# Attention block plus channel MLP on one Trainium2 core: the head rebuilt slice by slice, two chunks turned by transfers, the MLP from the loop's top, the last sums kept on chip

## The chip, the cores and the metric

The kernel runs on one core of a Trainium2 chip. TensorE (PE in the profile, PEld for its weight loads) multiplies matrices into PSUM, VectorE (DVE) and ScalarE (ACT) do the elementwise work, GpSimd (POOL) a few small things, SyncE (SP) issues nearly all transfers. The metric is the device time of one execution in microseconds, a median over runs; lower is better.

## The reference, cut to what matters

```python
xn = layernorm(x)                                  # x: 1 x 2048 x 640
q, k, v = split(xn @ wqkv)                         # 32 heads of 20
o = softmax(q @ k.T * 20**-0.5) @ v
y = layernorm(xn)                                  # a second norm, for the MLP
h = gelu(y @ w1 + b1)                              # 640 -> 1536, tanh form
out = x + o.reshape(2048, 640) @ wo + h @ w2 + b2  # 1536 -> 640
```

All inputs and outputs are float32. The kernel multiplies float32 numbers as sums of half-precision parts: each operand is split into a high f16 part and an f16 remainder, and three of the four products are added in PSUM (`PASS`).

## The kernel before, in words

**Head (L155 to L509).** The 2048 tokens are worked off in four chunks of 512, the features in five slices of 128. For chunk c: `load_x` brings four blocks of 128 tokens x 640; `norm_a` (L220) takes mean and variance with DVE and starts the inverse root on GpSimd (L233, a power of -0.5); `norm_b` (L236) refines the root by one Newton step (L215 to L218) and scales the rows (L243); `norm_c` finishes a second root for the MLP's own norm and stores it in `rscr`. `transp` (L256) turns the scaled rows on PE so that features lie on partitions; `transp_out` (L266) copies the high part with ACT (L269) and the remainder with DVE (L270) into `xnt`, which is also written to DRAM (`xscr`) for the MLP. `qk(c, tt)` (L277) multiplies 256 columns of q and k by the chunk, 30 matmuls (L286); tt runs from 0 to 4. `qk_out` (L293) scales and splits the result with ACT (L300) and DVE (L301), squares it for the row norms (L304, L306) and writes it to `qkscr`, from where the attention loop reads stacked heads. `lengths` (L313) sums the squares by head on PE (L321). `vproj` (L343) and `vproj_out` make the V rows, four products a chunk. Between these steps stands the preparation of the weights: `sums` (squares with ACT, L94), `scale_of` (a PE sum over partitions, L110, and a chain of small DVE operations that make a power of two), `split_qkv` (L379: high part ACT L382, remainder DVE L383). `some(n)` advances the same for the MLP's weights.

The order of all this is written out by hand (L444 to L509, `manual_schedule`): every engine executes its instructions in the order in which the code names them. Before the first product `warm(40)` and `warm(12)` keep PE busy with matmuls whose result is not used. The staging of q and v lies in the tile of w1 and that of k in the tile of w2, so the loads of w2 (L474) and w1 (L482) wait until those are split. Each transfer has one of eight semaphores in turn, and its issue waits for the transfer eight before it. SP issues in order too: what waits at its front holds all behind it.

**Attention loop (L963 to L1008).** For 16 pairs of heads, two halves of the queries, two columns of 512 and 16 blocks of 128 keys: `scores` (L594) makes two matmuls (L600) and one ACT exponential of 128 x 1024 (L602); `rest` subtracts the bf16 upper part for half of the blocks (L614); `pv` (L619) adds the products with V (L631), four blocks late. When a column is done ACT copies the sums out (L652) and `unload` (L660) writes them to DRAM (`opart`, and the row sums to `lpart`). `finish` (L683) reads back two or three pairs at a time, divides, splits and writes `oscr`.

PE's other work is woven in by a credit: once in every group of four key blocks (twice in the very first) the credit grows by `rate = 1.235` us, and `other()` (L970) takes steps from a generator until it is used up: first the MLP (`mlp`, L865: `layer1` L823, `gelu`, `layer2` L855), then the output projection (`projection`, L908, matmuls L932). The generator's first value is subtracted from the credit at the start:

```python
                credit = 0.0 - next(fill)        # L965
            load_chunk(0)                        # L866, in mlp()
            load_chunk(1)
            yield 2.0
```

`load_chunk` (L802) reads 256 tokens of `xscr` into a tile of the pool m2, which before exists only from the loop on, and broadcasts the MLP norm's factor (`r2f`). `tick` advances the side jobs, one step per call; a `yield` in a side job is one tick.

**Tail (from L1009).** After the last scores the rest of the projection runs, with one tick for every three matmuls. The last `finish` has its own form: a selection matmul (L735) spreads the inverse row sums over partitions; `W1 = 24` and `W2 = 17` ticks stand between its loads and the operations that use them. Projection pieces 4 to 7 need what it writes.

Of the kernel before, what the change touches and what calls it, by code (L numbers as in the profile page):

```python
# [42 lines left out]
def mha_mlp_kernel(tc, x, wqkv, wo, w1, b1, w2, b2, out):  # L43
# [4 lines left out]
    with (  # L48
# [3 lines left out]
        tc.tile_pool(name="st", bufs=2) as stp,  # L52
        tc.tile_pool(name="psS", bufs=3, space=PSUM) as psS,
# [99 lines left out]


        with tc.tile_pool(name="pa", bufs=2) as pa, tc.tile_pool(name="pa1", bufs=1) as pa1, tc.manual_schedule():  # L155
# [9 lines left out]
            def load_x(c):  # L165
                xts[c] = []
                for j in range(4):
                    xt = pa.tile([P, D], F32, tag="xt", name="xt", bufs=5)
                    nc.sync.dma_start(xt, x2[c * 512 + j * P : c * 512 + (j + 1) * P, :])
                    xts[c].append(xt)  # L170
# [7 lines left out]
            for q, n in enumerate("qkv"):  # L178
                if n == "v":
                    load_x(1)  # L180
                for k0, k1 in ((0, 3), (3, KD)):
                    nc.sync.dma_start(stage[n][:, k0:k1], wqkv_v[:, k0:k1, q * D : (q + 1) * D])
# [19 lines left out]
            brow = pa1.tile([H, S], F16, name="brow")  # L202
# [10 lines left out]
            def newton(dst, v, pref):  # L213
                t = pa.tile([P, 4], F32, tag=pref + "t", name=pref + "t")
                nc.vector.tensor_mul(t, dst, dst)  # L215
                nc.vector.tensor_mul(t, t, v)
                nc.vector.tensor_scalar(t, t, -0.5, 1.5, ALU.mult, ALU.add)
                nc.vector.tensor_mul(dst, dst, t)  # L218

            def norm_a(c):  # L220

                xt = xts[c]
                st = pa.tile([P, 4, 2, 6], F32, tag="st", name="st")
                mv = pa.tile([P, 4, 2], F32, tag="mv", name="mv")
                ve = pa.tile([P, 4], F32, tag="ve", name="ve")
                r = pa.tile([P, 4], F32, tag="r", name="r")
                r2 = pa.tile([P, 4], F32, tag="r2", name="r2")
                for j in range(4):
                    for i in range(2):
                        nc.vector.bn_stats(st[:, j, i, :], xt[j][:, i * 320 : (i + 1) * 320])  # L230
                    nc.vector.bn_aggr(mv[:, j, :], st[:, j])
                nc.vector.tensor_scalar(ve, mv[:, :, 1], EPS, None, ALU.add)
                nc.gpsimd.tensor_tensor(r, ve, nhalf, ALU.pow)  # L233
                rs[c] = mv, ve, r, r2

            def norm_b(c):  # L236
                mv, ve, r, r2 = rs[c]
                newton(r, ve, "a")

                nc.vector.tensor_mul(ve, r, r)  # L240
                nc.vector.tensor_scalar(r, r, 1024.0, None, ALU.mult)
                for j in range(4):
                    nc.vector.tensor_scalar(xts[c][j], xts[c][j], mv[:, j, 0:1], r[:, j : j + 1],  # L243
                                            ALU.subtract, ALU.mult)
                nc.vector.tensor_mul(ve, ve, mv[:, :, 1])
                nc.vector.tensor_scalar(ve, ve, EPS, None, ALU.add)
                nc.gpsimd.tensor_tensor(r2, ve, nhalf, ALU.pow)
# [8 lines left out]
            def transp(c, k0, pts):  # L256
                if k0 == 0:
                    xnts[c] = pa.tile([P, KD, 2, 512], F16, tag="xnt", name=f"xnt{c}")
                pt = psS.tile([P, 2, 512], F32, tag="s", name="pt")
                for j in range(4):  # L260
                    for k in range(min(2, KD - k0)):
                        nc.tensor.transpose(pt[:, k, j * P : (j + 1) * P],
                                            xts[c][j][:, (k0 + k) * P : (k0 + k + 1) * P], ident)
                pts.append((c, k0, pt))
# [9 lines left out]

            PASS = ((0, 0), (0, 1), (1, 0))

            def qk(c, tt):  # L277
                ps = psS.tile([P, 2, 512], F32, tag="s", name="qkp")
                order = [(i, k) for i in range(2) for k in range(KD)]
                if c + tt == 0:  # L280

                    order = [(i, k) for k in range(KD) for i in range(2)]
                for i, k in order:
                    q, mm = divmod(2 * tt + i, KD)
                    for n, (a, b) in enumerate(PASS):
                        nc.tensor.matmul(ps[:, i, :], wv[:, k, q, a, mm * P : (mm + 1) * P],  # L286
                                         xnts[c][:, k, b, :], start=(k + n == 0), stop=(k == KD - 1 and n == 2))
                return ps
# [4 lines left out]
            def qk_out(c, tt, ps):  # L293
# [3 lines left out]
                sq = pa.tile([P, 2, 512], BF16, tag="sq", name="sq", bufs=2)  # L297
                for i0, i1 in parts:
# [3 lines left out]
                                                   ALU.mult, ALU.subtract)  # L302
                if c == 0:
                    nc.scalar.activation(sq, hl[:, 0], AF.Square)  # L304
                else:
                    nc.vector.tensor_mul(sq, hl[:, 0], hl[:, 0])  # L306
                for s in range(2):
                    nc.sync.dma_start(
                        qkscr[s, 2 * tt * P : (2 * tt + 2) * P, c * 512 : (c + 1) * 512]
                        .rearrange("(i p) t -> p i t", p=P), hl[:, s])  # L310
                pend.extend((c, 2 * tt + i, sq[:, i]) for i in range(2))

            def lengths():  # L313

                for c, m, sq in pend:
# [10 lines left out]
                pend.clear()  # L326

            def shifts():
# [12 lines left out]
                nc.sync.dma_start(bscr[:H, :], brow)  # L341
# [37 lines left out]
            def split_qkv(n):  # L379
                q = "qkv".index(n)  # L380
                for k in range(KD):
                    nc.scalar.activation(wv[:, k, q, 0], stage[n][:, k], AF.Copy, scale=scales[n])  # L382
                    nc.vector.scalar_tensor_tensor(wv[:, k, q, 1], stage[n][:, k], scales[n], wv[:, k, q, 0],  # L383
                                                   ALU.mult, ALU.subtract)
# [59 lines left out]
            warm(40)  # L444
            norm_a(0)
            nc.gpsimd.memset(brow, KROW)
            sums("q", [stage["q"][:, 0:3], stage["q"][:, 3:]])
            norm_b(0)
            pts = []
            transp(0, 0, pts)  # L450
            scale_of("q")
            transp(0, 2, pts)
            transp(0, 4, pts)
            warm(12)
            for t in pts:
                transp_out(*t)
            split_qkv("q")
            nc.sync.dma_start(bscr[H : H + 1, :], brow[0:1, :])
            nc.sync.dma_start(b1t, b1.rearrange("(k p) -> p k", p=P))
            for c in range(4):  # L460
                nxt = c + 1 if c < 3 else None
                for tt in range(5):
                    ps = qk(c, tt)
                    lengths()

                    if c == 0:
                        if tt == 0:
                            sums("k", [stage["k"][:, 0:3], stage["k"][:, 3:]])
                            norm_c(0)
                            scale_of("k")  # L470
                        elif tt == 1:
                            split_qkv("k")
                            norm_a(1)
                            nc.sync.dma_start(w2t, w2.rearrange("(k p) n -> p k n", p=P))  # L474
                        elif tt == 2:
                            sums("v", [stage["v"][:, 0:3], stage["v"][:, 3:]])
                            norm_b(1)
                            scale_of("v")
                        elif tt == 3:
                            norm_c(1)  # L480
                            split_qkv("v")
                            nc.sync.dma_start(w1t, w1.rearrange("(k p) n -> p k n", p=P))  # L482
                    else:
                        if nxt and tt < 3:
                            (norm_a, norm_b, norm_c)[tt](nxt)
# [4 lines left out]
                    if nxt and tt >= 2:  # L490
                        pts = []
                        transp(nxt, 2 * (tt - 2), pts)
                        transp_out(*pts[0])
                if c + 2 < 4:
                    load_x(c + 2)
# [4 lines left out]
                for j in range(4):  # L500
                    ps = vproj(c, j)
                    lengths()
# [5 lines left out]
                    vproj_out(c, j, ps)  # L508
            some(99)  # L509


        with ExitStack() as scope:
# [3 lines left out]
            m2 = pool(name="m2", bufs=2)  # L516
# [143 lines left out]
            def unload(g, hf, ev):  # L660
                cols = slice(hf * 1024, (hf + 1) * 1024)
                for p in range(2):
# [12 lines left out]
            fins = []  # L675
# [7 lines left out]
            def finish(g0, g1, hf):  # L683
# [6 lines left out]
                yield  # L690
                for p in range(2):
                    go(lt[: nh * 16, p, :], lpart[p, hf, 2 * g0 : 2 * g1, :].rearrange("h (b t) -> (h b) t", t=64))
                for c0 in range(0, 1024, w):
# [18 lines left out]
                    o0, o1, rb = o0[: r1 - r0], o1[: r1 - r0], rb[: r1 - r0]  # L712
                    for p, o in enumerate((o0, o1)):
                        go(o, opart[p, r0:r1, cols])
# [87 lines left out]
            def load_chunk(mc):  # L802
                t0 = mc * MC
                xnt = m2.tile([P, KD, 2, MC], F16, tag="xnt", name="xm")
                r2f = m2.tile([P, MC], F32, tag="r2f", name="r2f")
                nc.sync.dma_start(xnt, xscr[:, :, :, t0 : t0 + MC])
# [58 lines left out]
            def mlp():  # L865
                load_chunk(0)  # L866
                load_chunk(1)
                yield 2.0
# [22 lines left out]
            def addup_out(ps, acc, t0, hf):  # L891
                cols = slice(hf * 320, (hf + 1) * 320)
                nc.vector.scalar_tensor_tensor(acc[:, cols], ps[:, :320], fo, acc[:, cols], ALU.mult, ALU.add)  # L893
                if hf == 1:
                    nc.sync.dma_start(out2[t0 : t0 + P, :], acc)
# [10 lines left out]
            W1, W2 = 24, 17  # L906
# [222 lines left out]
```

## Time and profile before

| | us |
|---|---|
| median of 3 runs (lowest, highest) | 1376.91 (1376.67, 1377.99) |
| time of the profiled execution | 1378.13 |
| its span | 1376.4 |
| PE, DVE, ACT busy in it | 1347.3, 1061.0, 1125.5 |
| first product of q (L286) starts | 21.02 |
| chunk 1, 2, 3 begin | 76.0, about 129, 182.3 |
| attention loop begins (first L600) | 232.72 |
| last PV product ends | about 1303 |
| last projection matmul ends | 1369.6 |

The profile is that of one execution; its times count from the start of its span. A group line gives line, engine, operation, output and inputs; a timeline line gives start and duration, and in brackets how long the engine had stood idle and what ended that. PE and DVE overlap, so shares do not add up. Two figures are of use throughout: 30 matmuls of `qk` take 6.6, a product of `vproj` 4.14.

### The profile page before, as it was taken

The page shows a single profiled execution, that of the slowest core. Times are in us where ns is not written, and L with a number is a line of the kernel's source. Part 1 is how long each engine was busy: PE and PEld are TensorE (multiplying, and loading weights), DVE is VectorE, ACT ScalarE, POOL GpSimd, SP SyncE. Part 2 cuts the span into 40 slices and gives each one's busy share as a digit, 9 for nine tenths or more (in the row PEclk, how much of TensorE's full clock was granted, in tenths as well). Part 3 has the DMA queues.
Part 4 walks back from the last instruction along what each step waited for, and adds up shares of the span by engine and source line. Part 5 has one row for each costly group of instructions (what it writes and reads, how often), then busy time and mean ns, then how long its engine had stood idle before and what let it go on. Part 6 is the DMA issues. An engine that isn't in the chain of part 4 may idle for free.

```text
span 1376.4 us, 29091 instructions
## 1 busy us (share of the span) xinstructions
PE 1347.3 (98%) x11711; PEld 599.3 (44%) x11711; DVE 1061.0 (77%) x1425; ACT 1125.5 (82%) x1282; POOL 32.6 (2%) x75
## 2 busy tenths in 40 slices
PE   8999998999999999999999999999999999999998
PEld 6555555443334333433343333343434434333375
DVE  6647753899778988788888778887978898898732
ACT  5644332999999999999999999999999999999700
POOL 2000000000000000000000000000000000000000
PEclk9999999999999999999999999999999999999999
DMA  9853413012113222213231123232123222244275
GB/s 266 226 187 115 99 58 114 3 33 62 52 38 100 81 76 68 70 47 82 67 99 40 47 66 89 64 83 62 41 57 113 73 76 77 65 135 119 89 235 177
DMA packets 92320, 125.68 MB, mean 91 GB/s; under 512 B 16905, under 2 KB 58569, under 8 KB 92178
## 3 DMA queue, kind: packets, MB, share of 16 engines
q1 hardware_dynamic: 89218, 117.14, 28.9%
q0 software_dynamic: 2304, 5.24, 2.2%
q8 instruction: 94, 1.54, 0.5%
q10 hardware_dynamic: 656, 1.36, 0.3%
q14 instruction: 48, 0.39, 0.1%
HBM read 80.84 MB, written 42.86 MB: 90 GB/s over the span
## 4 chain that ended last, share of the span: by engine, by line
PE 66%; DVE 8%; ACT 3%; DMA 2%; issue 2%; SPq 1%; DVEq 0%; ACTq 0%
PE o L631 26%; PE s L600 16%; PE py L855 11%; PE pu L823 9%; PE z L932 4%; DVE low L614 3%; ACT p L602 3%; DVE u L758 1%; DVE u L759 1%; DVE w L762 1%; DMA oscr<-oa 1%; DMA acc<-accscr 0%; DVE w L763 0%; DVE hT L770 0%; DVE u L768 0%
## 5 line engine op out<-in xcount | busy, mean ns | idle before, releaser
L602 ACT ACTIVATE p<-s 128x1024 f32<-128x1024 f32 x1024 | 973.9, 1043 | 46.2 <-PE s L600 38.9
L614 DVE TENSOR_TENSOR low<-p 128x1024 f16<-128x1024 f32 x512 | 610.6, 1218 | 162.4 <-ACT p L602 161.7
L631 PE MATMUL o<-p,vfull 128*32 128x512 bf16 (+1 forms) x4096 | 430.2, 493 | 0.0
L600 PE MATMUL s<-qs,ks 61*128 61x512 f16 x2048 | 317.3, 382 | 7.0 <-ACT p L602 5.5
L600 PEld LDWEIGHTS <-ks 61*128 61x128 f16 x2048 | 64.0, 94 | 294.4 <-issue 291.9
L823 PE MATMUL pu<-xm,w1t 128*128 128x256 f16 x1440 | 181.1, 275 | 3.8 <-DMA xm<-xscr 2.7
L855 PE MATMUL py<-w2t,hT 128*128 128x320 f16 x1152 | 178.6, 300 | 1.7 <-DVE u L758 1.1
L823 PEld LDWEIGHTS <-w1t 128*128 128x128 f16 x1440 | 131.5, 98 | 72.1 <-issue 57.8
L855 PEld LDWEIGHTS <-hT 128*128 128x128 f16 x1152 | 102.5, 98 | 89.3 <-issue 55.1
L286 PE MATMUL qkp<-xnt,wv 128*128 128x512 f16 x600 | 132.5, 379 | 0.2 <-DVE wv L383 0.2
L631 PEld LDWEIGHTS <-vfull 128*32 128x32 f16 x3072 | 60.4, 95 | 137.7 <-issue 106.3
L631 PE MATMUL o<-low,vfull 128*32 128x512 f16 x1024 | 103.5, 378 | 3.7 <-DVE low L614 3.7
L300 ACT ACTIVATE qkhl<-qkp,qks 128x1024 f16<-128x1024 f32 (+1 forms) x24 | 23.3, 971 | 82.9 <-PE qkp L286 65.4
L286 PEld LDWEIGHTS <-wv 128*128 128x128 f16 x600 | 58.1, 98 | 68.2 <-DVE wv L383 0.7
L631 PEld LDWEIGHTS o<-p,vfull 128*32 128x32 f32 x2048 | 62.1, 108 | 52.3
L932 PE MATMUL z<-w1t,ot 128*128 128x320 f16 x480 | 66.3, 299 | 1.4 <-DMA ot<-oscr 0.8
L349 PE MATMUL vp<-wv,xnt 128*128 128x320 f16 x480 | 66.6, 299 | 0.0
L932 PEld LDWEIGHTS <-ot 128*128 128x128 f16 x480 | 46.5, 98 | 21.9 <-issue 2.9
L349 PEld LDWEIGHTS <-xnt 128*128 128x128 f16 x480 | 46.5, 98 | 18.2
L893 DVE SCALAR_TENSOR_TENSOR acc<-z,sc,acc 128x320 f32<-128x320 f32 x32 | 17.5, 550 | 46.8 <-PE z L932 42.7
L301 DVE SCALAR_TENSOR_TENSOR qkhl<-qkp,qks,qkhl 128x1024 f16<-128x1024 f32 (+1 forms) x24 | 26.5, 1104 | 32.2 <-ACT qkhl L300 32.2
L652 ACT ACTIVATE ev<-o 128x512 f32<-128x512 f32 x64 | 39.5, 618 | 3.5 <-PE o L631 3.5
(168 smaller groups left out, 682.6 us busy)
## 6 DMA issues: line engine op xcount, KB each, us to landing
qkscr<-qkhl SPq DMA_DIRECT2D x40, 256.0 KB
opart<-ev SPq DMA_DIRECT2D x124, 80.0 KB
ks<-qkscr SPq DMA_DIRECT2D x120, 80.0 KB
qs<-qkscr SPq DMA_DIRECT2D x192, 40.0 KB
oa<-opart SPq DMA_DIRECT2D x32, 240.0 KB
xt<-in_A_x_dram SPq DMA_DIRECT2D x16, 320.0 KB
xscr<-xnt SPq DMA_DIRECT2D x4, 1280.0 KB
xm<-xscr SPq DMA_DIRECT2D x8, 640.0 KB
```

The source lines that it names most:

```text
L286: nc.tensor.matmul(ps[:, i, :], wv[:, k, q, a, mm * P : (mm + 1) * P], xnts[c][:, k, b, :], start=(k + n == 0), stop=(k == KD - 1 and n == 2))
L300: nc.scalar.activation(hl[:, 0, i0:i1], ps[:, i0:i1], AF.Copy, scale=a)
L301: nc.vector.scalar_tensor_tensor(hl[:, 1, i0:i1], ps[:, i0:i1], a, hl[:, 0, i0:i1], ALU.mult, ALU.subtract)
L349: nc.tensor.matmul(ps[:, hf, :320], xnts[c][:, k, a, j * P : (j + 1) * P], wv[:, k, 2, b, hf * 320 : (hf + 1) * 320], start=(n == 0), stop ...
L600: nc.tensor.matmul(ps[:, a, :], ks[64 * a : 64 * a + 61, kb * P : (kb + 1) * P], qs[64 * a : 64 * a + 61, cc * 512 : (cc + 1) * 512], star ...
L602: nc.scalar.activation(pt, ps, AF.Exp, scale=QS)
L614: nc.vector.tensor_sub(low, pt, upper(pt))
L631: nc.tensor.matmul(pv.o[32 * q : 32 * q + 32, :], src[:, v0 - PAD * (1 - q % 2) :][:, :32], t, start=q not in pv.begun, stop=last, skip_gr ...
L652: nc.scalar.activation(evs[g, hf][:, cc], pv.o, AF.Copy)
L823: nc.tensor.matmul(ps[:, i], w1v[:, k, (f + i) // 4, a, fo_ : fo_ + P], xnt[:, k, b, :], start=(n == 0), stop=(n == 3 * KD - 1))
L855: nc.tensor.matmul(ps[:, :320], hTs[mc][:, f, a, j * P : (j + 1) * P], w2v[:, f, b, hf * 320 : (hf + 1) * 320], start=(n == 0), stop=(n == ...
L932: nc.tensor.matmul(ps[:, :320], ot[:, k, a, j * P : (j + 1) * P], wov[:, k, b, h * 320 : (h + 1) * 320], start=(n == 0), stop=(n == 3 * KD ...
```

## The change

Seven things are edited.

1. The weights of q are loaded in five slices, and their squares are summed slice by slice. Chunk 0's root is a square root on ACT and a reciprocal on DVE in place of GpSimd's power; the factor 1024 moves into the Newton step; the second root's start is a function of its own (`norm_b2`) and comes later for chunk 0. The length row `brow` has a quarter of its size, is filled earlier and is repeated by the transfer that stores it.
2. Chunk 0 is turned block by block as its rows are scaled, with q's scale before the last block; then each feature slice is copied out and 256 columns of q's weights are split for it. The second product takes its features in the outer loop too, has k's scale in its middle, and the outputs of the first product and the other columns of q follow it; an exponential of one element stands ahead of these. `warm` is called with 37 and 5.
3. Chunk 1 is turned on PE between the V products of chunk 0. Chunks 2 and 3 are split as rows (ACT, DVE) and turned by eight transposing transfers from SP out of three row tiles in turn.
4. `lengths` runs twice a chunk (four entries, then up to ten), with the squares of odd products in another pool.
5. x blocks are loaded into tiles of the pool m2, which now exists from the start; the first two MLP inputs are loaded in chunk 3, and `mlp` yields 0.0 at its start.
6. The last pair's sums are not written to DRAM: `finish` reads them from the tile in SBUF with twelve transfers on ACT's queue (four of them the earlier pair's), and W1 and W2 are 12 and 9.
7. The last block of the output is stored in two halves, the first from ACT's queue.

```diff
-                    xt = pa.tile([P, D], F32, tag="xt", name="xt", bufs=5)
+                    if j % 2 == 0:
+                        pair = m2.tile([P, KD, 2, MC], F16, tag="xnt", name="xt").bitcast(F32)
+                        pair = pair.rearrange("p k s t -> p (k s t)")
+                    xt = pair[:, j % 2 * D : (j % 2 + 1) * D]
...
-                for k0, k1 in ((0, 3), (3, KD)):
+                for k0, k1 in ((k, k + 1) for k in range(KD)) if n == "q" else ((0, 3), (3, KD)):
...
-                nc.gpsimd.tensor_tensor(r, ve, nhalf, ALU.pow)
+                if c == 0:
+                    nc.scalar.activation(r, ve, AF.Sqrt)
+                    nc.vector.reciprocal(r, r)
+                else:
+                    nc.gpsimd.tensor_tensor(r, ve, nhalf, ALU.pow)
...
+            def turn(c, j):
+                if j == 0:
+                    xnts[c] = pa.tile([P, KD, 2, 512], F16, tag="xnt", name=f"xnt{c}")
+                xv = xts[c][j].rearrange("p (k n) -> p k n", k=KD)
+                row = pa.tile([P, KD, 2, P], F16, tag="row", name="row", bufs=3)
+                nc.scalar.activation(row[:, :, 0, :], xv, AF.Copy)
+                nc.vector.tensor_sub(row[:, :, 1, :], xv, row[:, :, 0, :])
+                nc.sync.dma_start(xnts[c].rearrange("p k s t -> p (k s) t")[:, :, j * P : (j + 1) * P],
+                                  row.rearrange("p k s n -> p (k s n)"), transpose=True)
+                if j == 3:
+                    nc.sync.dma_start(xscr[:, :, :, c * 512 : (c + 1) * 512], xnts[c])
+                    del xts[c]
...
-            warm(40)
+            warm(37)
             norm_a(0)
-            nc.gpsimd.memset(brow, KROW)
-            sums("q", [stage["q"][:, 0:3], stage["q"][:, 3:]])
+            sums("q", [stage["q"][:, k] for k in range(KD)])
             norm_b(0)
-            pts = []
-            transp(0, 0, pts)
-            scale_of("q")
-            transp(0, 2, pts)
-            transp(0, 4, pts)
-            warm(12)
-            for t in pts:
-                transp_out(*t)
-            split_qkv("q")
...
+            for j in range(4):
+                if j == 3:
+                    scale_of("q")
+                    pt.append(psM.tile([P, 512], F32, tag="m", name="pt4"))
+                for k in range(KD - 1):
+                    nc.tensor.transpose(pt[k][:, j * P : (j + 1) * P], xts[0][j][:, k * P : (k + 1) * P], ident)
+            for j in range(4):
+                nc.tensor.transpose(pt[4][:, j * P : (j + 1) * P], xts[0][j][:, 4 * P :], ident)
+            warm(5)
+            for k in range(KD):
+                nc.scalar.activation(xnts[0][:, k, 0, :], pt[k], AF.Copy)
+                nc.vector.tensor_sub(xnts[0][:, k, 1, :], pt[k], xnts[0][:, k, 0, :])
+                split_qkv("q", [k], 0, 2 * P)
...
+                    if c == 0 and tt == 1:
+                        norm_b2(0)
+                        norm_c(0)
+                        nc.scalar.activation(junk[:, :1], ones[:, :1], AF.Exp)
+                        ps = qk(0, 1, lambda: scale_of("k"))
+                        hl = qk_out(0, 0, first)
+                        split_qkv("q", c0=4 * P)
+                        split_qkv("k")
...
-                    if nxt and tt >= 2:
-                        pts = []
-                        transp(nxt, 2 * (tt - 2), pts)
-                        transp_out(*pts[0])
+                    if nxt and c > 0 and tt >= 2:
+                        for j in ((0,), (1, 2), (3,))[tt - 2]:
+                            turn(nxt, j)
+                    if c == 3 and tt == 2:
+                        early = [load_features(mc) for mc in range(2)]
...
+                        for k in ((), (0,), (2, 4), ())[j]:
+                            transp(1, k, pts)
...
+                direct.extend([ev] if (g, hf) == ORDER[-1] else [])
-                for p in range(2):
+                for p in range(0 if direct else 2):
...
-                yield 2.0
+                yield 0.0
...
-                if hf == 1:
+                if t0 + P == S:
+                    (nc.scalar, nc.sync)[hf].dma_start(out2[t0 : t0 + P, cols], acc[:, cols])
+                elif hf == 1:
...
-            W1, W2 = 24, 17
+            W1, W2 = 12, 9
```

## The prediction

> **What bounds the kernel now.** I read the shares of the engines first, then what TensorE (PE) waited for, then the timeline and the table of windows at the four places that the diff touches. Times are us from the start of the span.
>
> ```profile
> PE 1347.3 (98%) x11711; PEld 599.3 (44%) x11711; DVE 1061.0 (77%) x1425; ACT 1125.5 (82%) x1282; POOL 32.6 (2%) x75
> ```
>
> PE is busy 98% of the span. So time can only come from PE work that is taken out, from PE work that computes nothing (the warm-up before the first product), from waits of PE, and from slow PE clocks. The waits are few:
>
> ```profile
> PE s L600 <- ACT p L602: 5.5, 18, 0.6
> PE o L631 <- DVE low L614: 3.7, 7, 0.8
> PE pu L823 <- DMA xm<-xscr: 2.7, 1, 2.7
> PE pt L262 <- DVE xt L243: 2.6, 2, 2.2
> ...
> PE z L932 <- DMA ot<-oscr: 0.8, 1, 0.8
> ```
>
> Columns: total, times, longest. Three waits happen once, at the head (L262), at the top of the attention loop (L823) and in the tail (L932); the change works on all three. The head, by the timeline (start, duration, engine, line):
>
> ```profile
> 8.30 0.89 DVE L230 BATCH_NORM_STATS2 st<-xt 128x6 f32<-128x320 f32 x2 [0.65 <-DMA xt<-in_A_x_dram]
> ...
> 11.19 1.36 DVE L217 TENSOR_SCALAR at<-at 128x4 f32<-128x4 f32 x1
> ...
> 12.67 1.27 ACT L94 ACTIVATE junk<-w1t 128x1280 bf16<-128x1280 f32 x1
> ...
> 13.18 2.18 DVE L243 TENSOR_SCALAR xt<-xt,mv,r 128x640 f32<-128x640 f32 x4
> ...
> 15.89 0.43 PE L110 MATMUL mxp<-acc,ones 128*128 128x2 f32 x2
> ...
> 21.02 0.59 PE L286 MATMUL qkp<-xnt,wv 128*128 128x512 f16 x2
> ```
>
> The reader is to see that the first useful product starts at 21.02, that L217, a 0.16 us operation, took 1.36 while GpSimd filled brow, and that the sum over q's weights (L110) ran at 15.89 though ACT had its squares by 14.04: it stood behind transposes. The top of the loop:
>
> ```profile
> 237.57 1.44 PE L823 MATMUL pu<-xm,w1t 128*128 128x256 f16 x6 [2.68 <-DMA xm<-xscr]
> ...
> 239.00:243.00 4.00, 4.00 (x21) 1.80 (x20) 2.35 (x2) 1.94 (x2) 0.00 (x0) 0.50 0.44 123
> ```
>
> PE waits 2.68 for the MLP's first input, and the granted clock (third figure from the right) is 0.50 for the four us after.
>
> **Part by part.** Sums are against the profiled execution: span 1376.4, time 1378.13, which is 1.22 above the median 1376.91 of the runs shown. I subtract the gain from the median.
>
> *Head.* norm_a ends at 9.63 in both (it waits for x's last block). Root: L233 on GpSimd to the next DVE operation took 1.16. A root on ACT is not in the trace; the least row of that size is 0.17 to 0.20, the most is the GpSimd row; two small operations and their hand-over, 0.5. The fill is moved ahead and quartered, so L217 is 0.2 (1.2 less), and two operations of 0.2 move behind. Scaling then starts at 10.95 instead of 13.18 and ends at 13.15. Squares of q go in five slices: 128x1920 and 128x1280 follow each other in 1.92 and 1.37, so 0.82 for 640; five from 9.95 end at 14.05, as before. Now the sum over partitions runs at 14.1, not 15.89; its DVE chain took 16.36 to 17.45, now 14.6 to 15.7. Each feature slice then costs ACT 0.58 + 0.41 (copy, split of 256 columns, by 0.74 for 640) and DVE 0.69 + 0.41: 1.1 for PE's 6 x 0.222 = 1.33, so PE sets the pace from the first slice on, about 16.7. Product 1 ends at 23.4 instead of 28.05: **4.6 gained**. Cover: DVE's 1.1 below 1.33; without it 0.2 a slice.
>
> *Rest of chunk 0.* Product 2 needs q's next 256 columns (2.1 on each engine, done 23.3: just in time). Behind it ACT has k's squares 3.3, the exponential's table, the first output 1.11, five splits of 0.3 and k's five of 0.74; DVE ends these at about 35.9, PE wants the last at 36.6. The table load is 1.28 in the trace (0.82 to 2.10, nothing waiting behind it); I book 0.3 of stall on product 3.
> The Trainium skill ("ScalarE: Activation LUTs", What ACT_TABLE_LOAD costs) puts 1.38 of drain on top, 2.66 for a switch; the trace shows the 1.28 and cannot show the drain at an idle start. By the rule product 3 stalls 1.0 more, and the sum would be 14.3 instead of 15.3.
> w2's load still starts near 36 (k's split ends then) and product 2's output is written behind its 3.9 MB. Before, ACT's output of product 4 waited for that write until 54.52; PE now comes 4 earlier, so this wait is late next: output 4 at 54.5 frees its PSUM buffer at about 56.5, PE wants it at 55.3. Bounds 0 (the queue is drained sooner) to 1.6; I take 0.8. Chunk 1's transposes between V products wait about 0.3 for DVE's scaling. The three stalls make 1.4 in 48.8; before the same stretch was 47.85 (28.05 to 75.9): **0.9 lost**.
>
> *Chunks 2 and 3 transposed by DMA.* Forty PE transposes go: chunk 1 and 2 last (182.3 - 76.0) / 2 = 53.15 each, chunk 3, which has none, 232.7 - 182.3 = 50.4. **5.5 gained**. ACT and DVE get four row copies and subtractions (128x640) in place of the outputs: about 0.7 x 4 each, as before, in stages where ACT is half idle. The eight transfers, 320 KB each, are on SP's queue before the writes of products 4 and 5. The trace has none. At p us each, one after another, they are in time if 94 + 4p (first one issued at about 94) is below 123 (chunk 2 wanted), so if p is below 7.2. Nearest row: the piece loads of the tail, the same 320 KB, 4.24 from the first issue to the landing of two; at the 403 GB/s of 44 to 46 it would be 0.8; the far end is the 17 GB/s of 34 to 36, 19 us. I take 4.
> The Trainium skill ("DMA: Bandwidth & Descriptors", Latency and other measured facts) gives 261 GB/s for a transposing transfer, an estimate of 1.3 us each; no run here shows it yet, and the sum is the same.
>
> *Norm sums in two lots, length row quartered, x loads in the m2 pool.* Same matmuls; 8 take 0.23 either way: 0. The x loads wait for the same transposes as before.
>
> *Loop top.* The first two MLP inputs are loaded in chunk 3: their 1.3 MB take 3.3 at 400 GB/s, and the writes queued behind them have a 6.8 period to hide it. The wait of 2.68 goes, 0.5 with it for the scores behind; the half clock of 4 us gives 2.0 more if PE no longer stands still. A credit of 2.0 less puts 24 instead of 6 MLP matmuls in the first group, where PE would otherwise wait for ACT, and the order of instructions shows 447 projection matmuls after the last PV product instead of 462: that is this same 2.0, paid in the loop and returned in the tail. **5.2 gained**. Bounds: 2.7 (the wait alone) to 7.2.
>
> *Tail.* The wait of 0.76 at L932 goes with the write and read back of the last sums; twelve issues on ACT's queue at 0.45 bring the six row sums about 6 after the last PV product, and the matmuls that use them now stand 54 products (7.35) behind it instead of 90: 0.4 of stall. Final store in halves: the window 1371 to 1372 shows 1 us of data, half of it goes early: 0.5. **0.9 gained**.
>
> Sum: 4.6 - 0.9 + 5.5 + 5.2 + 0.9 = **15.3**; 1376.9 - 15.3 = **1361.6**.
>
> **Rivals.** (1) *The head's gain is taken back.* For it: ACT waited three times, 7.4 in all, for qkscr writes to land in chunk 0, and w2's and w1's loads do not move with PE. Against: PE is three PSUM buffers ahead. If w2's landing still sets chunk 0's end and the first products run at the 0.53 clock that 16 to 18 shows after a 2.2 us pause (1.7 dearer), the 4.3 of lead and that 1.7 are lost, 6 in all: 1367.6 (1364 to 1373). (2) *The loop takes its gain back.* ACT is 96% busy between 240 and 1200; if ACT, not PE, paces the loop, what PE finds at its top is idle again later. For it: the 5.5 of PE waiting for ACT. Against: ACT idles 40 there, PE 10.7. Then 2.7 of 5.2 stay: 1364. (3) *Slower: the transposing transfers.* Each us of p beyond 7.2 delays chunks 2 and 3 by 4 each, 8 in all; from p = 9.1 nothing is gained, from 9.5 it is slower; at 19 us it is 1456. For it: no row shows such a transfer, and the chunk's feature write queues behind all four on SP. Against: the nearest row is 4.24. (4) *It does not do what it says*: the early loads land late and PE waits as before, 1372.
>
> **Chances.** A change within 0.2% (2.8 us) could not be told from none. Forecast, 1356 to 1366 with (2) inside it: 0.62. Rival 1: 0.17. Rival 4: 0.04. Better than 1356: 0.05. Rival 3: 0.12, of which 0.02 faster still, 0.02 within 0.2% and 0.08 slower. Faster 0.89, same 0.03, slower 0.08. The range 1356 to 1371 leaves the far end of the transfers and the best case out.
>
> **What would show it.** First L286 product near 16.7 and its thirtieth near 23.4; chunk 0's last V product ending near 72; no PE wait at the first product of chunks 2 and 3 (a wait there proves the transfers late); chunks 1 to 3 at about 51; the loop starting near 222.5, with no wait for xm and no half clock behind it; no PE wait for ot in the tail; the last store after the last DVE operation half as long. A PE wait for row copies or qkscr in chunk 0, or the loop longer by what its top saved, would make the prediction wrong.

## The result, and the profile after

The median after is 1364.6 us over six runs (1360.54 to 1365.88), against 1377.45 over six runs of before measured beside them (1376.42 to 1382.32). The ratio is 0.9897, 95% interval 0.9879 to 0.9914: 14.2 us faster, between 11.8 and 16.7 (the two medians lie 12.9 apart). The forecast was 1361.6, a gain of 15.3. The profiled execution after took 1364.71, its span is 1363.0, 13.4 less than before's 1376.4.

The shares, from the page of after: PE has 12.2 less work, and its share has not moved.

```profile
PE 1335.1 (98%) x11651; PEld 591.6 (43%) x11651; DVE 1060.5 (78%) x1436; ACT 1129.6 (83%) x1305; POOL 30.2 (2%) x74
```

What PE waited for, after (total, times, longest):

```profile
PE s L680 <- ACT p L682: 6.5, 21, 1.2
PE o L711 <- DVE low L694: 4.3, 8, 0.9
PE qkp L322 <- DVE qkhl L338: 2.1, 1, 2.1
PE z L1024 <- DVE oa L837: 1.8, 1, 1.8
```

The waits for xm and for ot are gone, and that for the scaled rows is down from 2.6 to 0.2. Two single waits are new: product 5 of chunk 0 (L322) and a projection matmul in the tail (L1024). The head, by the timeline of after:

```profile
9.75 0.21 ACT L245 ACTIVATE r<-ve 128x4 f32<-128x4 f32 x1 [7.64 <-DVE ve L243]
...
10.59 0.17 DVE L228 TENSOR_SCALAR at<-at 128x4 f32<-128x4 f32 x1
...
10.99 2.18 DVE L255 TENSOR_SCALAR xt<-xt,mv,r 128x640 f32<-128x640 f32 x4
...
14.17 0.39 PE L111 MATMUL mxp<-acc,ones 128*128 128x5 f32 x2 [0.81 <-ACT junk L95]
...
16.43 0.81 PE L322 MATMUL qkp<-xnt,wv 128*128 128x512 f16 x3
```

L228 (L217 before), which had taken 1.36, takes 0.17; the scaling starts at 10.99 instead of 13.18; the sum over q's partitions no longer stands behind transposes, but behind ACT's squares; the first product starts at 16.43 (forecast 16.7). Where it starts also depends on when x arrives: in all ten runs with this head it comes 6.89 or 6.90 behind the start of `norm_a`'s last DVE operation (`ve<-mv`, here 9.54), against 11.56 in before, so the head itself is worth 4.7. Product 5 of chunk 0, from PE's timeline of after:

```profile
42.95 0.38 PE L111 MATMUL mxp<-acc,ones 128*128 128x2 f32 x2
45.47 8.34 PE L322 MATMUL qkp<-xnt,wv 128*128 128x512 f16 x30 [2.14 <-DVE qkhl L338]
53.65 8.31 PE L395 MATMUL vp<-wv,xnt 128*128 128x320 f16 x60
```

It waits 2.14 and then takes 8.34 instead of the 6.65 of a product at full clock; the granted clock is 0.50 from 46.22 to 49.63. The wait hangs on ACT's output of product 3, which stands until 42.44 for the first write of `qkscr` to land; product 4's output stands for the second until 54.59 (ACT's timeline):

```profile
42.44 0.69 ACT L337 ACTIVATE qkhl<-qkp,qks 128x512 f16<-128x512 f32 x1 [2.82 <-DMA qkscr<-qkhl]
54.59 1.11 ACT L337 ACTIVATE qkhl<-qkp,qks 128x1024 f16<-128x1024 f32 x1 [4.43 <-DMA qkscr<-qkhl]
```

Where the span went, with all runs of the experiments (start of the first product; first product to chunk 1; chunks 1 to 3; first score to the end of the last PV product; from there to the end), all from PE's timelines:

| run | first | chunk 0 | 1 | 2 | 3 | loop | tail | span |
|---|---|---|---|---|---|---|---|---|
| before | 21.02 | 54.98 | 53.65 | 52.65 | 50.43 | 1070.46 | 73.21 | 1376.4 |
| after | 16.43 | 56.78 | 50.04 | 49.67 | 49.77 | 1067.67 | 72.64 | 1363.0 |
| e1_pe_turn | 15.88 | 56.46 | 52.36 | 51.90 | 49.77 | 1067.64 | 75.29 | 1369.3 |
| e2_loop_late | 15.99 | 54.72 | 50.04 | 49.67 | 49.77 | 1065.40 | 73.41 | 1359.0 |
| e3_lengths_each | 16.31 | 61.20 | 51.82 | 50.34 | 50.43 | 1067.60 | 72.90 | 1370.6 |
| e4_v_sum_psum | 16.32 | 56.25 | 50.04 | 49.67 | 49.77 | 1067.61 | 72.54 | 1362.2 |
| e5_rows_later | 15.60 | 52.82 | 52.92 | 49.67 | 49.77 | 1067.65 | 72.37 | 1360.8 |
| e6_b1_later | 15.55 | 53.18 | 50.03 | 49.68 | 49.77 | 1067.64 | 72.55 | 1358.4 |
| e7_tail | 15.52 | 58.46 | 50.04 | 49.67 | 49.77 | 1067.94 | 71.70 | 1363.1 |
| e8_pow_root | 15.64 | 55.31 | 50.03 | 49.68 | 49.77 | 1067.71 | 72.36 | 1360.5 |
| e9_pool_late | 15.68 | 56.06 | 50.04 | 49.67 | 49.77 | 1070.40 | 72.88 | 1364.5 |
| b1_best | 15.77 | 53.63 | 50.04 | 49.67 | 49.77 | 1065.37 | 73.05 | 1357.3 |

Read it by columns. Chunks 1 to 3 repeat to 0.01 and the loop to 0.11 wherever their code is the same (the loop but for 0.3 in one run), so a difference there is an effect of the edit even in one profile. The first product comes at 15.5 to 16.4 with the same head, and chunk 0 takes 54.7 to 58.5 with the same code (after, e1, e2, e7, e9): there one profile proves nothing under 4 us, and there lies the wider spread of after's times. Of the whole times of the experiments, only those of e1 and e3 have intervals that are clear of after's; the others show what they show in their columns.

Before to after: 4.59 at the first product, -1.80 in chunk 0, 7.25 in chunks 1 to 3 (3.61, 2.98, 0.66), 2.79 in the loop, 0.57 in the tail: 13.40.

### The profile page after: what moved, and what is told of

Read it like the earlier page. It is cut to its first block, busy times and chain, and to the rows that moved or that the text cites. A ratio compares the mean times of both kernels' runs of the same rounds, so it can differ in the third digit from the quotient of the medians.

```text
span 1363.0 us, 29029 instructions
## 1 busy us (share of the span) xinstructions
PE 1335.1 (98%) x11651; PEld 591.6 (43%) x11651; DVE 1060.5 (78%) x1436; ACT 1129.6 (83%) x1305; POOL 30.2 (2%) x74
## 2 busy tenths in 40 slices
DMA packets 103073, 127.94 MB, mean 94 GB/s; under 512 B 27516, under 2 KB 69568, under 8 KB 102932
## 4 chain that ended last, share of the span: by engine, by line
PE 79%; DVE 9%; ACT 7%; issue 3%; DMA 2%; ACTq 0%; SPq 0%; DVEq 0%
PE o L711 26%; PE s L680 17%; PE py L945 11%; PE pu L913 9%; PE qkp L322 8%; PE vp L395 5%; ACT p L682 4%; PE z L1024 4%; DVE low L694 3%; DMA oa<-ev 1%; DVE u L849 1%; DMA qkscr<-qkhl 1%; DVE u L850 1%; DVE w L853 1%; DVE w L854 1%
## 5 line engine op out<-in xcount | busy, mean ns | idle before, releaser
L322 PE MATMUL qkp<-xnt,wv 128*128 128x512 f16 x600 | 132.7, 383 | 2.3 <-DVE qkhl L338 2.1
L322 PEld LDWEIGHTS <-wv 128*128 128x128 f16 x600 | 58.7, 99 | 73.2 <-issue 2.6
L1024 PE MATMUL z<-w1t,ot 128*128 128x320 f16 x480 | 66.7, 300 | 1.8 <-DVE oa L837 1.8
L1024 PEld LDWEIGHTS <-ot 128*128 128x128 f16 x480 | 46.3, 98 | 23.1 <-issue 2.9
L983 DVE SCALAR_TENSOR_TENSOR acc<-z,sc,acc 128x320 f32<-128x320 f32 x32 | 17.5, 550 | 43.2 <-PE z L1024 39.9
```

What stands on the lines that cost most here:

```text
L1024: nc.tensor.matmul(ps[:, :320], ot[:, k, a, j * P : (j + 1) * P], wov[:, k, b, h * 320 : (h + 1) * 320], start=(n == 0), stop=(n == 3 * KD ...
```

## The experiments

The theory was that the gain is a sum of independent places and that its two shortfalls are product 5 and the tail's transfers; each run undoes or alters one place.

**Chunks 2 and 3 turned on PE.**

```diff
-                        for j in ((0,), (1, 2), (3,))[tt - 2]:
-                            turn(nxt, j)
+                        pts = []
+                        transp(nxt, 2 * (tt - 2), pts)
+                        transp_out(*pts[0])
```

> Chunks 2 and 3 are turned on PE again, two slices behind each of products 2 to 4, all else as after. Theory (the gain is a sum of independent places, and these forty transposes are worth what PE spends on them): chunks 1 and 2 last 53.1 each again instead of 50.0 and 49.7, chunk 3 stays at 49.8, the span is 6 to 7 us longer (1369 to 1370). Rival (the transposing transfers hold other work back on SP's queue, so that part of their gain is lost somewhere behind): less than 4 us longer, and chunk 3 or the loop's top shorter than after's.

Ratio 0.995 (0.9933 to 0.9967), median 1371.01. Chunks 1 and 2 grow by 2.32 and 2.23, not by 3: the transposes were worth 4.55 (PE spends 4.66 on the forty in before, from their starts to the next product's). Nothing is given back behind them, so the rival falls. The tail is 2.65 longer in this profile, by a wait of 2.89 in place of 1.79 for the same DVE line, with the clock at 0.54 and 0.61 for the 4 us behind it; nothing in the edit touches the tail. The medians of this run and after lie 6.4 apart, and the chunks explain 4.55 of it; whether the other executions have the longer tail too is not shown.

**The norm sums in small lots.**

```diff
-                    if tt == 3:
-                        lengths(4)
+                    lengths(99)
...
-                    if j == (0 if c == 3 else 1):
-                        lengths(10)
+                    lengths(99)
```

> The norm sums run in five small lots a chunk, behind every product, as before, instead of two. Theory: each chunk from 1 to 3 is 0.65 longer (chunk 3 was 50.4 with five lots and is 49.8 with two): about 2 us over three chunks, 1365 in the profile. Rival (chunk 3's 0.65 came from elsewhere, such as the squares in two pools or fewer waits of PE): chunks 1 to 3 unchanged within 0.2.

Ratio 0.9947 (0.9925 to 0.9968), median 1372.07. Chunks 1 to 3 grow by 1.78, 0.67 and 0.66: 3.1. In chunk 3, where PE waits for nothing, five lots take 1.14 instead of 0.79 and the products between them 0.30 more; chunk 1 has a wait of 0.96 for squares besides. Chunk 0 takes 61.2, 2.7 over the longest with after's code. PE's timeline of this run (in brackets: idle time, and what ended it):

```profile
46.41 0.40 PE L367 MATMUL norms<-sq,heads 128*32 128x128 bf16 x8 [3.17 <-ACT sq L354]
...
57.97 0.30 PE L367 MATMUL norms<-sq,heads 128*32 128x128 bf16 x8 [1.54 <-ACT sq L354]
```

With every product followed by its small lot, PE stands at squares that ACT has not made yet; with two lots PE waits for no square in after. So the lots are more than 8 matmuls in another place: in chunk 0 they let PE run on when outputs are late, as far as one profile shows it.

**The loop's top, first try.**

```diff
-                        early = [load_features(mc) for mc in range(2)]
+                        early = []
...
-                yield 0.0
+                yield 2.0
```

> The loop's top is as before the change: the MLP's first two inputs are loaded at the loop's top and the credit begins 2.0 lower. Theory: PE waits about 2.7 for xm at its first MLP matmul, runs at the 0.50 clock for about 4 us behind it, and the time from the first score to the last PV product grows from 1067.6 to about 1070.4, with 15 projection matmuls (2.04) more left for the tail: 4.8 in all. Rival (ACT paces the loop, so the loop takes the gain back): the sum is 1.5 to 3 only.

Ratio 0.9895 (0.9875 to 0.9916), median 1362.51: not slower. The expectation missed. PE does not wait for xm: with the pool there from the start, the program's order puts one of the two loads into chunk 2 by itself (SP issues it at 153.64) and the other ahead of the first scores (215.34). So this run tells of the credit alone: the loop is 2.27 shorter than after's, the tail only 0.77 longer, although it has the 15 projection matmuls (2.04) back.

**The loop's top, second try: the pool too.**

```diff
-        tc.tile_pool(name="m2", bufs=2) as m2,
...
-                        pair = m2.tile([P, KD, 2, MC], F16, tag="xnt", name="xt").bitcast(F32)
+                        pair = m2a.tile([P, KD, 2, MC], F16, tag="xnt", name="xt").bitcast(F32)
...
+            m2 = pool(name="m2", bufs=2)
```

(m2a is a pool of the head; the two edits of the first try are kept.)

> The pool of the MLP's inputs is made at the loop's start again (the x blocks have a pool of their own that ends there), the explicit early loads are left out and the credit begins 2.0 lower: the loop's top is as before the change. The run without the explicit early loads kept one load early by itself and lost nothing, so this one is the test that it was meant to be. Theory: PE waits 2.7 for xm at its first MLP matmul, has 0.50 of its clock for some 4 us behind it, and the stretch from the first score to the last PV product is 1070.4 again, against 1065.4 in that run and 1067.7 in after. Rival (ACT paces the loop): 1068 or less.

Ratio 0.9907 (0.9875 to 0.9938), median 1366.72; the loop takes 1070.40. PE's timeline of this run, then its windows (granted clock third from the right):

```profile
226.17 1.44 PE L913 MATMUL pu<-xm,w1t 128*128 128x256 f16 x6 [2.78 <-DMA xm<-xscr]
```

```profile
224.00:228.00 4.00, 1.83 (x10) 0.83 (x9) 1.34 (x2) 1.70 (x2) 0.00 (x0) 0.66 1.03 266
228.00:232.00 4.00, 4.00 (x20) 1.74 (x16) 2.36 (x2) 2.11 (x3) 0.00 (x0) 0.50 0.45 111
```

Against the first try, with the same credit, the loop is 5.00 longer: wait and half clock, as forecast (5.2), and the loop does not take it back. The rival falls.

**Another PSUM tile for v's sum.**

```diff
-            if tag in ("q", "k"):
+            if tag in ("q", "k", "v"):
```

> The sum over partitions for v's scale takes the one-bank PSUM tile that q's and k's take, instead of one of the three buffers that the products use. Theory (product 5 of chunk 0 waits only because this sum took a buffer, so that it needs the output of product 3, which waits for the landing of the first qkscr write): the wait of 2.1 at 45.5 goes, the product takes 6.65 instead of 8.34, and chunk 0 ends 3 to 3.8 us earlier. Rival (the next output that waits for a landing, w2's, sets the end of chunk 0 all the same): the wait moves to the V products and 0 to 1 us is gained.

Ratio 0.9894 (0.9874 to 0.9914), median 1363.77. Product 5 starts at 43.07 and takes 6.63, but (PE's timeline):

```profile
49.54 4.24 PE L395 MATMUL vp<-wv,xnt 128*128 128x320 f16 x30
56.46 4.25 PE L395 MATMUL vp<-wv,xnt 128*128 128x320 f16 x30 [2.68 <-DVE qkhl L338]
```

The rival is right: the wait moves to the second V product, which needs product 4's output, and that stands behind w2's load. The buffer was the place of the stall, the landings its cause.

**What delays the landings.** In after, data hardly moves from 32 to 40, and before had the same gap (77 and 47 GB/s). The windows of after (last column GB/s):

```profile
32.00:36.00 4.00, 4.00 (x20) 1.80 (x19) 3.57 (x5) 3.97 (x5) 0.00 (x0) 1.00 1.56 51
36.00:40.00 4.00, 4.00 (x20) 1.83 (x19) 3.90 (x12) 3.59 (x5) 0.00 (x0) 1.00 0.65 53
40.00:44.00 4.00, 3.33 (x31) 1.53 (x29) 1.58 (x5) 0.74 (x2) 1.01 (x1) 1.00 0.91 266
```

w2's load is issued at 34.99, and data flows again from 41. Issued shortly before are two transfers in pieces of 4 bytes, b1 (1536) and the factors (512). One run moves each away.

```diff
-                nc.sync.dma_start(rscr[c * 512 : (c + 1) * 512].rearrange("(j p) -> p j", p=P), r2)
+                rows = lambda: nc.sync.dma_start(rscr[c * 512 : (c + 1) * 512].rearrange("(j p) -> p j", p=P), r2)
+                if c == 0:
+                    late.append(rows)
...
                     load_x(2)
+                    late.pop()()
```

> The write of chunk 0's second-norm factors to rscr (512 pieces of 4 bytes) is issued behind chunk 0 instead of at 26, all else as after. Theory (these pieces, not w2's load, keep the queues from moving data between 30 and 40: 57 GB/s there, and after the same write of chunk 2 at 103 as well): data flows at over 200 GB/s in 32 to 40, the first qkscr write lands before 36, w2 lands before 50, product 5 of chunk 0 waits for nothing, chunk 1 begins at 70 to 70.5 instead of 73.2: 2.5 to 3 us faster. Rival (b1's load of 1536 such pieces does it, or the writes themselves): the landing moves by less than 2 and product 5 still waits.

```diff
-            nc.sync.dma_start(b1t, b1.rearrange("(k p) -> p k", p=P))
             for c in range(4):
...
                     load_x(2)
+                    nc.sync.dma_start(b1t, b1.rearrange("(k p) -> p k", p=P))
```

> The load of b1 (1536 pieces of 4 bytes) is issued behind chunk 0 instead of at 25; the rscr write stays. Theory of the rscr write: the gap between 30 and 40 stays for the most part, as 4-byte writes were followed by one in chunk 2 without any b1 load. Rival (the 1536 pieces of b1 are the larger part): the first qkscr write lands 5 us or more earlier, and chunk 1 begins at 70 to 70.5.

The same window 36 to 40, first without the factors, then without b1:

```profile
36.00:40.00 4.00, 4.00 (x21) 1.81 (x19) 3.83 (x14) 3.33 (x5) 0.00 (x0) 1.00 1.00 383
```

```profile
36.00:40.00 4.00, 4.00 (x20) 1.85 (x19) 3.83 (x14) 3.29 (x5) 0.00 (x0) 1.00 0.93 293
```

Theory and rival are both half right: each of the two adds to the gap, and taking either away gives 383 or 293 GB/s in this window, where the eight runs that keep both in place have 20 to 161 (after 53). Chunk 0 takes 52.82 and 53.18, under the 54.7 to 58.5 of after's code, and PE waits for none of its q and k products there. Moving the factors gives 1363.09 (0.9881, 0.9851 to 0.9912), moving b1 1361.09 (0.9867, 0.9836 to 0.9898); both intervals overlap after's. The former is less since the late write meets chunk 1: 2.9 longer there, with a wait of 1.62 for product 5's buffer. The gap from 32 to 36 stays in both (20 and 66 GB/s). Why such pieces hold back what is issued behind them stays open.

**The tail.**

```diff
-            W1, W2 = 12, 9
+            W1, W2 = 12, 17
```

(And the last block is stored in one piece.)

> Tail: 17 instead of 9 ticks between the loads of the last sums and the addition (W2), and the last block is stored in one piece. Theory (DVE's addition stands 9 ticks behind transfers that need 11, so that PE, which waits for a projection result read by DVE behind it, loses 1.8; halving the store gains nothing): the PE wait of 1.8 at the projection goes and no wait for ot takes its place, the tail is 71 instead of 72.6, and the end from the last DVE operation to the span's end stays at 6.2. Rival 1: the later oscr write makes PE wait for ot by 0.8 or more, the tail stays over 72. Rival 2: the end is 0.5 longer than 6.18.

Ratio 0.9861 (0.9831 to 0.9892), median 1360.98, though the profile was of its longest run, with chunk 0 at 58.46; the edit itself is the tail: 71.70, 0.94 less. The wait for DVE is gone and one of 0.67 for ot stands in its place (rival 1 in part). From DVE's last operation to the end it is 6.5 against 6.2 in after. But before, which also stores the last block in one piece, has 6.2 there too (1370.22 to 1376.4), so it is not shown that the halves are worth anything.

**The root on GpSimd.**

```diff
-                if c == 0:
+                if c == -1:
                     nc.scalar.activation(r, ve, AF.Sqrt)
```

> Chunk 0's root is GpSimd's power again (1.04 before), all else as after; no table for the square root. Theory (the root on ACT saves about 0.6 of the head's chain: 0.56 from the end of DVE's L243 to the reciprocal's end, against 1.16): scaling of the rows starts 1.7 to 1.8 behind the end of the last L243 instead of 1.3 (9.71 to 10.99), the first product 0 to 0.6 later, and the table load at the exponential stays where it is or goes to the start. Rival (the squares of q on ACT, which stand behind the square root in its order, set the first product): the squares start 0.2 earlier without it and the first product comes no later or up to 0.3 earlier; then the root on ACT was worth nothing. Either way under 0.7 us in all.

Ratio 0.9901 (0.9884 to 0.9917), median 1362.49. The timeline of this run:

```profile
8.39 0.74 ACT L95 ACTIVATE junk<-w1t 128x640 bf16<-128x640 f32 x1 [6.29 <-DMA w1t<-in_A_wqkv_dram]
...
8.95 0.17 DVE L243 TENSOR_SCALAR ve<-mv 128x4 f32<-128x4 f32 x1
9.21 1.04 POOL L248 TENSOR_TENSOR r<-ve,nhalf 128x4 f32<-128x4 f32 x1 [1.44 <-DVE ve L243]
...
15.64 1.03 PE L322 MATMUL qkp<-xnt,wv 128*128 128x512 f16 x4
```

The squares start before the root and not behind it. From the start of L243 to the first product it is 6.69, in after 6.89 (9.54 to 16.43), as in every run with that head. Counted from there too, the scaling starts 2.14 behind with GpSimd's root instead of 1.45, but the squares end 3.73 behind instead of 4.58. The rival is right: in ACT's order the root stood ahead of what sets the first product, and saved nothing. The second table load goes with it.

**Three edits together.** b1 later, v's sum in the other tile, `yield 2.0`.

> After with three edits from the runs: b1 loaded behind chunk 0, v's sum in the one-bank PSUM tile, and the credit at the loop's top 2.0 lower as before the change (the explicit early loads stay). Theory (places are independent): chunk 1 begins at 68.5 to 69, the loop lasts 1065.4 and the tail 73.4, so that the span is about 1357 (18.5 from the first product on, 1358.7 as time), 0.9863 of before. Rival (the credit is not what made the loop 2.3 shorter in the run without the explicit early loads, but the place of the loads): the loop lasts 1067.6 and the span is 1358.4 or more. What would tell nothing new: the same 1361 as the run with b1 later.

Median 1359.76 (1358.97 to 1360.0, four runs), ratio 0.9879 (0.9862 to 0.9895). The explicit loads are kept and the loop takes 1065.37, so the credit makes the 2.3, not the place of the loads. Its interval overlaps after's; its four runs all lie under the lowest of after's six, but were measured beside other runs of before (median 1376.5), and e6 and e7 have lower ratios still. That it is faster than after is likely, and shown only for the loop. In its list of waits the tail has left:

```profile
PE z L1024 <- DMA ot<-oscr: 0.2, 1, 0.2
```

## Why the prediction was right, and where it was not

The sum was 15.3, the profiles give 13.4. The mechanism held at the head, in the chunks and at the loop's top, where PE's named waits are gone. But four terms were off, and two of them cancel: the norm sums gave 2.7 where 0 stood, and loop and tail together 2.7 less than forecast. That the sum came so near is luck in that part. Two figures of the forecast do not follow from its own terms: they put the loop's start at 223.5 and not 222.5 (it came at 222.69), and the loss of the loop top alone would give 1366.8 and not the 1372 of rival 4.

- *Head, 4.6.* First product at 16.43 and the end of its thirtieth at 23.08 (forecast 16.7 and 23.4): about 5, 4.6 of it at the start of the product and 0.4 as it now runs without a break. Size right, one reason wrong: the 0.5 for a root on ACT in place of 1.16 bought nothing, as the sum over q's partitions then waits for ACT's squares. The fill moved ahead, the slices and the order of the transposes did it.
- *Rest of chunk 0, -0.9.* It was -2.2 (50.1 from the end of product 1 to chunk 1, against 47.95 and a forecast of 48.8); the same code gives from -0.1 (e2) to -3.9 (e7), so the size is one draw of a wide spread. The 0.3 for the table load did not come: products 2 to 4 run without a break past it. Product 4's output did wait until 54.59, as forecast (54.5). What was missed stands one product earlier: v's sum takes one of three product buffers, so product 5 waits for the first qkscr write, 2.14, and for 1.7 of half clock. The argument "PE is three PSUM buffers ahead" counted a buffer that was not free. A PE wait that hangs on qkscr in chunk 0 was one of the named signs of being wrong; it came, and the stretch lost 1.3 more than was booked.
- *Table load.* ACT's timeline of after:

```profile
25.86 1.28 ACT L522 ACT_TABLE_LOAD   x1
27.15 0.20 ACT L522 ACTIVATE junk<-ones 128x1 bf16<-128x1 f32 x1
```

The next operation starts 1.29 behind the load's start and ACT was busy up to 25.78, so the switch cost 1.4 and not the 2.66 by the Trainium skill ("ScalarE: Activation LUTs", What ACT_TABLE_LOAD costs): the drain of 1.38 is not to be seen here.

- *Transposing transfers, 5.5.* Worth 4.55. The taking of chunk 3 as "a chunk without transposes" mixed in what differs otherwise. SP is held 1.33 to 2.23 by six of the eight issues and 4.53 and 8.26 by the other two; the feature write, which waits for the last landing, follows the last issue by 5.4 and 3.5 (estimates of p from above; 4 was taken). Rival 3 had no part: PE waits at no first product of chunks 2 and 3.
- *Norm sums, 0.* The mis-sized term that saved the forecast: 3.1 in chunks 1 to 3 in the run that undoes it, and 2.7 of the 7.25 that they gained is left for it beside the 4.55. It was put at nothing because the matmuls are the same; that small lots take longer, they and the products between them, and that PE can wait for squares, was not counted. In chunk 0 it is a guard as well.
- *Loop top, 5.2, and tail, 0.9.* Together 3.36 instead of 6.1. Wait and half clock were worth 5.0, as forecast. The failed step is "paid in the loop and returned in the tail": the credit costs 2.27 in the loop, and the tail cannot return it, because those 15 matmuls were its cover. DVE's timeline of after, then PE's, then the chain that ended last:

```profile
1306.40 1.22 DVE L835 TENSOR_TENSOR oa<-oa 80x1024 f32<-80x1024 f32 x1 [2.75 <-DMA oa<-ev]
1307.65 1.22 DVE L837 TENSOR_TENSOR oa<-oa,rb 80x1024 f32<-80x1024 f32 x1
1308.79 0.54 DVE L983 SCALAR_TENSOR_TENSOR acc<-z,sc,acc 128x320 f32<-128x320 f32 x1
```

```profile
1308.93 3.30 PE L1024 MATMUL z<-w1t,ot 128*128 128x320 f16 x23 [1.79 <-DVE oa L837]
```

```profile
1294.98 5.30 DMA oa<-ev
1300.28 0.02 issue
1300.31 5.90 DMA oa<-ev
```

DVE stands 2.75 at the addition; the sum that frees PE's buffer (L983) is queued behind it. The addition waits for the last of the twelve transfers, which was issued only when the first direct read of features (from 1294.98) had landed. The row sums are used from 1296.68, 6.3 behind the last PV product, as forecast (about 6); it is the direct reads' landings, 15.9 behind it, that the forecast left out. With the credit as in before the tail takes 72.88, 73.05 and 73.41 (e9, b1_best, e2) against 73.21, so the edits of the tail by themselves are worth nothing that can be told. Loop and tail together are 1143.67 before, 1140.31 after, 1138.42 in b1_best. The 0.5 for the halved store is not shown: the end takes 6.2 before and after.

None of the rivals came as a whole. Of rival 1 (6 lost in chunk 0) about a third came, by a mechanism near its own: a late landing and a slow clock behind it, at product 5 and not at the first products.

## What to carry to other kernels

A matmul that is moved out of one place is cover taken from the transfers there: look at what it hid before calling the move neutral. Where an output waits for a write to land, look at which buffers are really free (small helpers take them too) and at the pieces of the transfers issued before it; two of 8 KB in all held up a load of 4 MB here: product 4's output came 36.1 to 39.9 behind the first product with both in place, and 34.2 and 34.6 with one or the other moved. Where two lists of work are due, give PE the older one: a lot of sums that waits for nothing is worth more than its matmuls.

## What the runs showed that was not expected

PE's clock was 0.50 behind pauses of 2.08 and 2.89 (e1), 2.14 (after), 2.62 (e7), 2.78 (e9) and 3.17 (e3), not behind 1.62 (e5), 1.79 (after's tail), and not behind 2.68 between V products (e4): length alone does not decide it. The Trainium skill ("TensorE: Matmul & The Clock Gate", Part 1) has the clock fall after an idle window of about 3.4 that runs freely. The traces agree with such windows: each half clock in the middle of the span lasts 3.41 or 6.83, twice that, and the two of e1 start at 44.40 and 1314.15, 372 times 3.413 apart. But a window need not be idle throughout. Laid out from these starts, the seven windows at full clock with 63 to 85% of PE idle (two of them in before) were each followed by half clock, and those with up to 53% were not (after's 1.79 fills 52% of one window, e4's 2.68 is shared out as 25 and 53%). One does not fit, 48% in front of e1's 2.08, and where between 53 and 63% the point lies is not shown. The half clock went on for a second window in the three cases in which the first had 22 to 36% idle.

So where a pause of 2 to 3 falls in a window would decide, as between e4's 2.68 and e7's 2.62 (74% of one window). The two direct reads in the chain above move 20 rows of 4 KB each from SBUF into SBUF; 5.30 and 5.90 are from issue to landing. The transposing transfers move in pieces of 256 bytes: pieces under 512 bytes rose from 16905 to 27516 in the pages.
